# Attention and MLP on one core: score groups of each batch moved up by two groups, and the last half product cut in two column pieces

## The chip, the core and the metric

The kernel runs on one core of a Trainium2 chip. The core has five engines that run side by side, each with its own instruction queue worked in order: TensorE (PE) multiplies matrices into PSUM, VectorE (DVE) and ScalarE (ACT) work on PSUM and SBUF, GpSimd (POOL) casts here, and SyncE (SP) issues most of the DMAs. A DMA that SP, ACT or POOL issues waits in that engine's queue until what it reads is there, and holds all behind it. Times are device microseconds; the metric is the time of one execution.

## What is computed

```python
B, H, S, D = 8, 12, 448, 64
scores = q @ k.transpose(0, 1, 3, 2) / sqrt(D)
attn = softmax(scores)
x = (attn @ v).transpose(0, 2, 1, 3).reshape(B * S, H * D)
h = x @ w_in
g = maximum(0.01 * h, h)
out = g @ w_out
```

The inputs q, k, v (8 x 12 x 448 x 64), w_in (768 x 2048) and w_out (2048 x 768) and the output (3584 x 768) are float32. The kernel multiplies in bfloat16.

## The kernel before

**Units and groups.** The attention is cut into 48 units; unit u is one pair of heads of one batch, so six units make a batch. A unit has four chunks of 112 keys. For a chunk, `scores(u, c)` (L252) does two matmuls into one of three PSUM tiles `sc`, and `expo(u, c)` (L261) is one ACT instruction that writes the exponentials into one of three buffers `e`. `pv(u, j)` (L271) then multiplies the exponentials of head j with v in 16 matmuls, and DVE divides by the row sums (L278, L279) into a tile `x`. When both heads of a unit are done, `x_transposes(u)` turns the tile into the rows of `xT` that the MLP reads; from unit 9 on this is a DMA transpose on SP's queue (L213). Likewise the casted q and k of a unit (L146, on POOL) are turned into `qkT` by a DMA transpose from unit 14 on.

`cluster(g)` is a group: three chunks of scores, their exponentials (the third is held in `late` until the next call of `settle()`), the heads that are due, and the casts, loads and transposes of later units. Four groups are three units, so a batch has eight groups. `cluster` is called with `free` true or false; with false it places no heads and leaves them in `due`.

**Token ranges.** The MLP runs over eight ranges of tokens, i = 0 to 7, cut at multiples of 128: 384 tokens for even i, 512 for odd i. Range i needs `xT` of all of batch i. `mlp(i)` yields its steps one after the other: 16 input products (`part`, L326, six matmuls each, accumulated over the 128-row slices of `xT`, one slice per unit of the batch; ACT's leaky ReLU at L462 reads the bank), and then the output products. These are, for a pair of 128-token blocks, seven half-width products of eight matmuls (`block_pair`, L367; DVE prepares sums of h and of w_out, seven products take the place of eight), and for an odd block two full products (`blocks`, L427). Input and output products and `pv` share two PSUM banks, `g`, in turn (`next_bank`). In `block_pair` the two tiles `a` and `b` are these banks.

**What sets the order.** The order is written by hand; each engine's queue is what the loop at the end emits. `begin[i]` is the first group that is placed inside range i, and the groups `begin[i]` to `begin[i + 1] - 1` are spread over its steps in proportion to the matmul columns done (`catch_up`), after steps that yield true or false, not after those that yield None. So `begin` alone says how far the attention runs ahead of the MLP: batch i ends with group 8(i + 1) - 1, and range i starts in front of group `begin[i]`:

```python
begin = [9] + [8 * (i + 1) + 3 for i in range(1, B)]
```

The values are 9, 19, 27, 35, 43, 51, 59, 67: ten groups in range 0, eight in each of 1 to 6. The groups 64 to 66 have no scores, only heads that are due.

**Start of the last range.** For i = 7 two input products (m = 0 and m = 8) are opened ahead, five of six matmuls each, one in either bank (L456 to L458), and the first two steps add the sixth (L461).

**The end.** The very last product of the last block pair, the other half of block `o2`, is done in two pieces of 192 columns (L401 to L408), each followed by a DVE copy and two stores, one on ACT's queue (16 rows) and one on SP's (112 rows).

Of the kernel before, what the change touches and what calls it, by code (L numbers as in the profile page):

```python
# [16 lines left out]
def kernel(  # L17
# [11 lines left out]
    B, H, S, D = q.shape  # L29
# [5 lines left out]
    KD = DM // P  # L35
    MD = DF // P
    NW = DM // 2
# [3 lines left out]
    cuts = [((b * S) // P) * P for b in range(B)] + [B * S]  # L41
# [22 lines left out]
    def next_bank():  # L64

        banks.reverse()
        return banks[1]
# [19 lines left out]
    w_out_sb = w_pool.tile([P, MD, DM], BF16)  # L87
    MH = MD // 2
# [130 lines left out]
    def idle_slot():  # L219

        t = ps_s.tile([P, 2, 512], F32, name="sc", tag="sc")
        return t[:, 0], t[:, 1]
# [36 lines left out]
    def expo(u, c):  # L259
        e = e_sb[u % NE][:, :EL].rearrange("p (j c s) -> p j c s", j=2, c=NSC)  # L260
        nc.scalar.activation(e[:, :, c, :], sc_t.pop((u, c))[:SC, :, :S], AX.Exp, scale=scale)  # L261
# [34 lines left out]
    def store(o, t0, cols=slice(0, DM), queues=(nc.sync, nc.sync)):  # L296

        queues = list(queues)
        done = 0
        while done < P:  # L300
            b, j = divmod(t0 + done, S)
            so, p = divmod(j, SC)
            n = min(SC - p, P - done)
            dst = out[b * S:(b + 1) * S].rearrange("(p so) n -> so p n", so=NSC)
            queues.pop(0).dma_start(out=dst[so, p:p + n, cols], in_=o[done:done + n, cols])
            done += n
# [4 lines left out]
    def settle():  # L311
        while late:
            expo(*late.pop(0))

    open_t = {}
    opened = (0, 1)

    def part(i, m, kks, bank=None):

        n = cuts[i + 1] - cuts[i]  # L320
        at = cuts[i] % NX
        fresh = m not in open_t
        if fresh:
            open_t[m] = next_bank() if bank is None else bank
        for kk in kks:
            nc.tensor.matmul(  # L326
                open_t[m][:, :n], w_in_sb[:, kk, ts(m, P)], xT[:, kk, at:at + n],
                start=(fresh and kk == kks[0]), stop=(kk == KD - 1),
            )

    def mix_weights():

        for m in range(0, MH, 2):
            lo, hi = slice(m, m + 2), slice(MH + m, MH + m + 2)
            w11, w12 = w_out_sb[:, lo, :NW], w_out_sb[:, lo, NW:]
            w21, w22 = w_out_sb[:, hi, :NW], w_out_sb[:, hi, NW:]
            t1, t2, t3, t4 = (w_mix[:, x, lo] for x in range(4))
            for o, x, y in ((t1, w12, w11), (t2, w22, t1), (t3, w22, w12), (t4, w21, t2)):
                nc.vector.tensor_sub(o, x, y)
                yield  # L340

    def mix_h(h, m, nh):

        lo, hi = slice(m, m + 2), slice(MH + m, MH + m + 2)
        h11, h21 = h[:, lo, :nh], h[:, lo, nh:2 * nh]
        h12, h22 = h[:, hi, :nh], h[:, hi, nh:2 * nh]
        s2, s3, s4 = (h_mix[:, x, lo, :nh] for x in range(3))
        nc.vector.tensor_sub(s3, h11, h21)  # L348
        nc.vector.tensor_add(h21, h21, h22)
        nc.vector.tensor_sub(s2, h21, h11)  # L350
        nc.vector.tensor_sub(s4, h12, s2)

    def block_pair(i, h, c, nh):

        lo, hi = slice(0, MH), slice(MH, MD)
        one, two = ts(c, P), slice(nh + c * P, nh + (c + 1) * P)
        s2, s3, s4 = (h_mix[:, x, :, one] for x in range(3))
        t1, t2, t3, t4 = (w_mix[:, x] for x in range(4))
        left, right = slice(0, NW), slice(NW, DM)
        o1 = o_pool.tile([P, DM], F32, name="o")  # L360
        o2 = o_pool.tile([P, DM], F32, name="o")
        b, a = next_bank(), next_bank()

        def product(ps, x, w, first=False):
            settle()
            for m in range(MH):
                nc.tensor.matmul(  # L367
                    ps[:, :NW], x[:, m], w[:, m], start=(first and m == 0), stop=(m == MH - 1), skip_group_check=True,
                )
            return MH * NW  # L370

        def keep(o, at, ps):
            nc.vector.tensor_copy(o[:, at], ps[:, :NW])  # L373

        def join(o, at, ps):
            nc.vector.tensor_add(o[:, at], o[:, at], ps[:, :NW])  # L376

        done = product(b, h[:, lo, one], w_out_sb[:, lo, left], first=True)
        keep(o1, left, b)
        yield done, None  # L380
        done = product(a, h[:, hi, one], w_out_sb[:, hi, left], first=True)
        join(o1, left, a)
        yield done, None
        done = product(b, s2, t2)
        keep(o1, right, b)
        yield done, None
        done = product(a, h[:, lo, two], t1, first=True)
        keep(o2, right, a)
        yield done, False
        done = product(b, s3, t3)  # L390
        join(o2, right, b)
        yield done, None
        done = product(a, s4, w_out_sb[:, hi, right])
        join(o1, right, a)
        store(o1, cuts[i] + one.start)
        yield done, None
        t0 = cuts[i] + two.start
        if t0 + P == B * S:
            store(o2, t0, right)
            settle()  # L400
            for w in (slice(0, NW // 2), slice(NW // 2, NW)):  # L401
                for m in range(MH):
                    nc.tensor.matmul(  # L403
                        b[:, w], h[:, MH + m, two], t4[:, m, w], start=False, stop=(m == MH - 1),
                        skip_group_check=True,
                    )
                nc.vector.tensor_copy(o2[:, w], b[:, w])
                store(o2, t0, w, (nc.scalar, nc.sync))  # L408
        else:
            done = product(b, h[:, hi, two], t4)  # L410
            keep(o2, left, b)
            store(o2, t0)
        next_bank()
        yield done, True

    def blocks(i, h, todo):

        o = {}
        n = cuts[i + 1] - cuts[i]
        for c, w in todo:  # L420
            settle()
            if c not in o:
                o[c] = o_pool.tile([P, DM], F32, name="o")
            ps = next_bank()
            nw = w.stop - w.start
            for m in range(MD):
                nc.tensor.matmul(  # L427
                    ps[:, :nw], h[:, m, ts(c, P)], w_out_sb[:, m, w],
                    start=(m == 0), stop=(m == MD - 1),
                )  # L430
            nc.vector.tensor_copy(o[c][:, w], ps[:, :nw])
            t0 = cuts[i] + c * P
            if w.stop == DM:
                store(o.pop(c), t0)
            yield MD * nw, True

    def mlp(i):

        n = cuts[i + 1] - cuts[i]
        h = h_pool.tile([P, MD, 4 * P], BF16, name="h")  # L440
        if i == 0:
            for m in opened:
                part(i, m, (KD - 1,))
            for m in range(MD):
                if m not in opened:
                    part(i, m, range(KD))
                nc.scalar.activation(h[:, m, :n], open_t.pop(m)[:, :n], AX.Prelu, alpha=0.01)
                settle()
                yield KD * n, True
            yield from blocks(i, h, [(c, slice(w, w + NW)) for w in (0, NW) for c in range(n // P)])  # L450
            return

        nh = n // (2 * P) * P
        weights = mix_weights() if i == 1 else iter(())
        ready = []
        if i == B - 1:  # L456
            for m in (0, MH):
                part(i, m, range(KD - 1))  # L458
        for m in range(MD):
            mm = m // 2 + m % 2 * MH  # L460
            part(i, mm, (KD - 1,) if mm in open_t else range(KD))  # L461
            nc.scalar.activation(h[:, mm, :n], open_t.pop(mm)[:, :n], AX.Prelu, alpha=0.01)  # L462
            settle()
            if ready:
                mix_h(h, ready.pop(), nh)
            if m % 4 == 3:
                ready.append(m // 2 - 1)
            next(weights, None)
            yield KD * n, True
        mix_h(h, ready.pop(), nh)  # L470
        for c in range(2 * nh // P, n // P):
            yield from blocks(i, h, [(c, slice(0, NW)), (c, slice(NW, DM))])
        for c in range(nh // P):
            yield from block_pair(i, h, c, nh)
# [90 lines left out]
    a, b = idle_slot()  # L565
# [16 lines left out]
    cast(HP + 3)  # L582


    begin = [9] + [8 * (i + 1) + 3 for i in range(1, B)]

    early = [4, 6, 8, 10, 12, 14, 16, 18, 20, 22]
    for i in range(B):
# [6 lines left out]
        used, done, groups = 0, 0, 0  # L595
# [50 lines left out]
```

## Time and profile before

| | |
|---|---|
| median of three runs | 418.79 us (417.53 to 420.53) |
| the profiled execution, its own time | 418.34 us |
| its span, first to last instruction | 416.6 us |
| mean granted clock of TensorE | 0.992 |
| instructions in the span | 9157 |
| HBM read, written | 45.61 MB, 11.01 MB |

The profile is one execution. A row of the timeline gives start and length in us, engine, line, operation, out<-in with shapes, the count of instructions merged into it, and in brackets how long the engine was idle before and which instruction released it. Matmuls are pipelined and the end of one is modelled, so the length of a row of matmuls holds the drain of the last one; the chain of waits counts the pace alone. PEld is the load of a matmul's weights, which overlaps with matmuls. SPq and ACTq are the queues of those engines, where DMAs are issued.

### The profile page before, as it was taken

To read this page: it belongs to the slowest core of one execution; us is meant where nothing else is said; L and a number is where in the kernel's file an instruction comes from. 1 tells how busy PE (TensorE), PEld (TensorE's weight loads), DVE (VectorE), ACT (ScalarE), POOL (GpSimd) and SP (SyncE) were. 2 spreads that over 40 slices of the span, in tenths; PEclk is the share of its full clock that TensorE was granted. 3 is DMA by queue.
4 is the path that set the end of the run, shared out by engine and by line. 5 is a ranking of instruction groups with operands and counts; after the bars stand their busy time and mean duration, and the time that the engine had idled before them with its cause. 6 is when DMAs were issued, how large, how long until landed. Compare 5 with 4: busy or idle time off the path is not lost.

```text
span 416.6 us, 9157 instructions
## 1 busy us (share of the span) xinstructions
PE 397.6 (95%) x3672; PEld 228.8 (55%) x3672; DVE 170.1 (41%) x457; ACT 228.4 (55%) x324; POOL 109.0 (26%) x177
## 2 busy tenths in 40 slices
PE   8899999999998999989999799999999899999994
PEld 3566665645565666544555556554555456654463
DVE  2652433366543334423544234334344324333442
ACT  5998773576424884457542686447643388114300
POOL 8776655541112221311211313131211000000000
PEclk9999999999999999999999999999999999999998
DMA  8999999983558847862659848877356511130022
GB/s 127 198 201 204 202 199 115 245 199 89 134 161 187 183 112 171 221 145 70 166 130 194 172 100 189 206 186 122 101 124 175 121 35 24 49 89 0 2 76 76
DMA packets 96587, 57.23 MB, mean 137 GB/s; under 512 B 53281, under 2 KB 93089, under 8 KB 96545
## 3 DMA queue, kind: packets, MB, share of 16 engines
q1 hardware_dynamic: 76848, 44.15, 46.1%
q0 software_dynamic: 19392, 12.26, 20.6%
q8 instruction: 28, 0.46, 0.4%
q10 hardware_dynamic: 304, 0.25, 0.2%
q14 instruction: 15, 0.11, 0.1%
HBM read 45.61 MB, written 11.01 MB: 136 GB/s over the span
## 4 chain that ended last, share of the span: by engine, by line
PE 88%; DMA 7%; DVE 2%; issue 1%; POOL 1%; ACT 0%; DVEq 0%; ACTq 0%; POOLq 0%
PE g L326 34%; PE g L367 24%; PE g L271 11%; PE sc L252 9%; PE g L427 8%; DMA xT<-x 4%; DMA fk<-in_k_dram 2%; PE g L235 1%; DMA out_dram<-o 1%; DVE x L279 1%; PE g L292 1%; PE sc L326 0%; DVE rec L278 0%; PE g L403 0%; POOL fq L111 0%
## 5 line engine op out<-in xcount | busy, mean ns | idle before, releaser
L261 ACT ACTIVATE e<-sc 112x896 bf16<-112x896 f32 x192 | 165.7, 916 | 89.1 <-PE sc L252 88.6
L326 PE MATMUL g<-xT,w_in_sb 128*128 128x512 bf16 (+1 forms) x756 | 151.5, 354 | 9.5 <-DMA xT<-x 7.8
L326 PEld LDWEIGHTS <-w_in_sb 128*128 128x128 bf16 x768 | 72.9, 98 | 75.4 <-issue 12.3
L462 ACT ACTIVATE h<-g 128x512 bf16<-128x512 f32 (+1 forms) x112 | 61.7, 552 | 69.6 <-PE g L326 69.0
L271 PEld LDWEIGHTS <-e 112*128 112x128 bf16 x1536 | 56.4, 98 | 23.3 <-issue 14.8
L271 PE MATMUL g<-v,e 112*128 112x65 bf16 x1536 | 64.3, 195 | 0.3 <-ACT e L261 0.2
L278 DVE RECIPROCAL rec<-g 112x4 f32<-112x4 f32 x96 | 17.5, 182 | 80.5 <-PE g L271 52.0
L252 PE MATMUL sc<-qkT 64*128 64x448 bf16 x384 | 49.8, 356 | 0.4 <-DVE qkT L241 0.4
L146 POOL CAST qkb<-fq 112x512 bf16<-112x512 f32 x30 | 19.5, 651 | 116.0 <-DMA fq<-in_q_dram 69.7
L367 PEld LDWEIGHTS <-h 128*128 128x128 bf16 x344 | 33.5, 98 | 23.1 <-issue 1.2
L279 DVE TENSOR_TENSOR x<-g,rec 112x256 bf16<-112x256 f32 x96 | 40.8, 425 | 3.6 <-DVE rec L278 0.3
L148 POOL CAST v<-fv 112x512 bf16<-112x512 f32 x30 | 18.7, 622 | 71.7 <-PE g L271 62.6
L373 DVE COPY o<-g 128x384 f32<-128x384 f32 x43 | 24.0, 557 | 30.2 <-PE g L367 30.2
L367 PEld LDWEIGHTS <-hmix 128*128 128x128 bf16 x264 | 25.2, 98 | 19.4 <-issue 3.6
L427 PE MATMUL g<-w_out_sb,h 128*128 128x384 bf16 x192 | 32.5, 326 | 0.4 <-DVE x L279 0.3
L367 PE MATMUL g<-w_mix,hmix 128*128 128x384 bf16 x176 | 32.3, 326 | 0.0
L367 PE MATMUL g<-w_out_sb,h 128*128 128x384 bf16 x176 | 30.4, 326 | 0.8 <-DVE x L279 0.7
L367 PE MATMUL g<-w_mix,h 128*128 128x384 bf16 x168 | 30.7, 326 | 0.0
L376 DVE TENSOR_TENSOR o<-o,g 128x384 f32<-128x384 f32 x33 | 18.3, 554 | 28.4 <-PE g L367 28.4
L427 PEld LDWEIGHTS <-h 128*128 128x128 bf16 x192 | 18.5, 98 | 12.2 <-issue 0.5
L252 PEld LDWEIGHTS <-qkT 64*128 64x128 bf16 x384 | 13.9, 94 | 18.8 <-issue 9.5
L348 DVE TENSOR_TENSOR hmix<-h 128x512 bf16<-128x512 bf16 (+1 forms) x28 | 10.5, 376 | 30.2 <-ACT h L462 30.2
(50 smaller groups left out, 198.2 us busy)
## 6 DMA issues: line engine op xcount, KB each, us to landing
fk<-in_k_dram SPq DMA_DIRECT2D x31, 224.0 KB, 3.5
fq<-in_q_dram SPq DMA_DIRECT2D x30, 224.0 KB, 3.3
fv<-in_v_dram SPq DMA_DIRECT2D x30, 224.0 KB, 4.0
w_in_sb<-in_moe_w_in_dram POOLq DMA_DIRECT2D x4, 768.0 KB, 11.6
w_out_sb<-in_moe_w_out_dram POOLq DMA_DIRECT2D x4, 768.0 KB, 13.4
out_dram<-o SPq DMA_DIRECT2D x7, 336.0 KB, 3.3
out_dram<-o SPq DMA_DIRECT2D x8, 288.0 KB, 3.1
out_dram<-o SPq DMA_DIRECT2D x8, 240.0 KB, 3.1
```

The lines of the kernel that those rows point to most:

```text
L146: by(qk_sb[u][:, x].rearrange("p so h d -> p h so d"), f)
L148: by(v_sb[u % NV][:, :, :, :D], f)
L252: nc.tensor.matmul(ps[:, j, :S], t[j * D:(j + 1) * D, S + c * SC:S + c * SC + P], t[j * D:(j + 1) * D, :S], start=True, stop=True,)
L261: nc.scalar.activation(e[:, :, c, :], sc_t.pop((u, c))[:SC, :, :S], AX.Exp, scale=scale)
L271: nc.tensor.matmul(ps[:, qc, :], e[:, at:at + P], vt[:, j, c, :], start=(c == 0), stop=(c == NSC - 1),)
L279: nc.vector.tensor_mul(x_t[u][:, :, j, :], ps[:SC, :, :D], rec.to_broadcast([SC, NSC, D]))
L326: nc.tensor.matmul(open_t[m][:, :n], w_in_sb[:, kk, ts(m, P)], xT[:, kk, at:at + n], start=(fresh and kk == kks[0]), stop=(kk == KD - 1),)
L367: nc.tensor.matmul(ps[:, :NW], x[:, m], w[:, m], start=(first and m == 0), stop=(m == MH - 1), skip_group_check=True,)
L373: nc.vector.tensor_copy(o[:, at], ps[:, :NW])
L376: nc.vector.tensor_add(o[:, at], o[:, at], ps[:, :NW])
L427: nc.tensor.matmul(ps[:, :nw], h[:, m, ts(c, P)], w_out_sb[:, m, w], start=(m == 0), stop=(m == MD - 1),)
L462: nc.scalar.activation(h[:, mm, :n], open_t.pop(mm)[:, :n], AX.Prelu, alpha=0.01)
```

## The change

```diff
@@ block_pair
-        done = product(a, s4, w_out_sb[:, hi, right])
-        join(o1, right, a)
-        store(o1, cuts[i] + one.start)
-        yield done, None
         t0 = cuts[i] + two.start
         if t0 + P == B * S:
             store(o2, t0, right)
-            settle()
-            for w in (slice(0, NW // 2), slice(NW // 2, NW)):
+
+            def piece(w):
+                settle()
                 for m in range(MH):
                     nc.tensor.matmul(
                         b[:, w], h[:, MH + m, two], t4[:, m, w], start=False, stop=(m == MH - 1),
                         skip_group_check=True,
                     )
+
+            def put(w):
                 nc.vector.tensor_copy(o2[:, w], b[:, w])
                 store(o2, t0, w, (nc.scalar, nc.sync))
-        else:
-            done = product(b, h[:, hi, two], t4)
-            keep(o2, left, b)
-            store(o2, t0)
+
+            piece(slice(0, NW // 2))
+            put(slice(0, NW // 2))
+            done = product(a, s4, w_out_sb[:, hi, right])
+            join(o1, right, a)
+            store(o1, cuts[i] + one.start)
+            piece(slice(NW // 2, NW))
+            put(slice(NW // 2, NW))
+            return
+        done = product(a, s4, w_out_sb[:, hi, right])
+        join(o1, right, a)
+        store(o1, cuts[i] + one.start)
+        yield done, None
+        done = product(b, h[:, hi, two], t4)
+        keep(o2, left, b)
+        store(o2, t0)
         next_bank()
         yield done, True
@@ mlp
-        if i == B - 1:
-            for m in (0, MH):
-                part(i, m, range(KD - 1))
         for m in range(MD):
             mm = m // 2 + m % 2 * MH
-            part(i, mm, (KD - 1,) if mm in open_t else range(KD))
+            part(i, mm, range(KD))
@@ the loop at the end
-    begin = [9] + [8 * (i + 1) + 3 for i in range(1, B)]
+    begin = [9, 8 * 2 + 3] + [8 * (i + 1) + 5 for i in range(2, B - 1)] + [8 * B + 3]
```

`begin` is now 9, 19, 29, 37, 45, 53, 61, 67. Range 1 holds ten groups (19 to 28) where it held eight, ranges 2 to 5 hold eight each, all two groups further on, and range 6 holds six (61 to 66). The two products opened ahead of range 7 are gone. The last block pair's order becomes: left piece, the product for the other block, right piece.

**The end of range 1 on SP's queue.** `x_1951` is unit 17, the last of batch 2, which range 2 reads, and `x_2105` is unit 18; `o_1965` and `o_1966` are the output blocks of the second block pair of range 1. Before:

```order
L305 DMA out_0_dram<-o_1965 48x768 [waits DMAHW1_49,DVE_49]
L305 DMA out_0_dram<-o_1965 80x768 [waits DMAHW2_49]
L305 DMA out_0_dram<-o_1966 16x768 [waits DMAHW3_49,DVE_49]
L305 DMA out_0_dram<-o_1966 112x768 [waits DMAHW4_49]
L213 DMA_TRANSPOSE xT_114<-x_1951 128x4x112 [waits DMAHW5_49,DVE_49]
L213 DMA_TRANSPOSE xT_114<-x_2105 128x4x112 [waits DMAHW6_49,DVE_49]
```

After, on the same queue, unit 17 is `x_1962`, unit 18 is `x_2025`, and the second block pair's stores begin with `o_2071`:

```order
L213 DMA_TRANSPOSE xT_114<-x_1962 128x4x112 [waits DMAHW5_49,DVE_49]
L122 DMA fq_2001<-in_q_dram 112x2x256 [waits DMAHW6_49]
L122 DMA fk_2003<-in_k_dram 112x2x256 [waits DMAHW7_49]
L122 DMA fv_2005<-in_v_dram 112x2x256 [waits DMAHW0_49,Pool_49]
L213 DMA_TRANSPOSE qkT1_111<-qkb_1904 128x8x112 [waits DMAHW1_49,PE_49,Pool_49]
L213 DMA_TRANSPOSE xT_114<-x_2025 128x4x112 [waits DMAHW2_49,DVE_49]
L122 DMA fq_2064<-in_q_dram 112x2x256 [waits DMAHW3_49]
L122 DMA fk_2066<-in_k_dram 112x2x256 [waits DMAHW4_49]
L122 DMA fv_2068<-in_v_dram 112x2x256 [waits DMAHW5_49,Pool_49]
L213 DMA_TRANSPOSE qkT2_112<-qkb_1997 128x8x112 [waits DMAHW6_49,PE_49,Pool_49]
L213 DMA_TRANSPOSE qkT3_113<-qkb_2060 128x8x112 [waits DMAHW7_49,PE_49,Pool_49]
L305 DMA out_0_dram<-o_2071 48x768 [waits DMAHW0_49,DVE_49]
```

Unit 17's transpose moved from behind the stores of the second block pair to a place ahead of them, and unit 18's with it; the loads of two units and two transposes of q and k moved up in the same way.

**Between the two block pairs of range 1 on PE.** Of each run of matmuls the first row is shown; `sc` is a chunk's scores, `e` and `v` the product of a head, L367 the block pairs. Before, after the first block pair:

```order
L271 MATMUL g1_100<-v4_105,e1_108 128x65 [waits Pool_49]
L252 MATMUL sc_1904<-qkT2_112 128x448 [waits Activation_49]
L252 MATMUL sc_1907<-qkT2_112 128x448 [waits Activation_49]
L252 MATMUL sc_1910<-qkT2_112 128x448 [waits Activation_49]
L271 MATMUL g0_99<-v4_105,e1_108 128x65 [waits DVE_49]
L271 MATMUL g1_100<-v5_106,e2_109 128x65 [waits Pool_49]
L367 MATMUL g0_99<-w_out_sb_116,h_1455 128x384 [waits DVE_49]
```

After, at the same place:

```order
L271 MATMUL g1_100<-v5_106,e2_109 128x65 [waits Pool_49]
L252 MATMUL sc_1966<-qkT2_112 128x448 [waits Activation_49]
L252 MATMUL sc_1969<-qkT3_113 128x448 [waits Activation_49]
L252 MATMUL sc_1972<-qkT3_113 128x448 [waits Activation_49]
L271 MATMUL g0_99<-v5_106,e2_109 128x65 [waits DVE_49]
L271 MATMUL g1_100<-v0_101,e0_107 128x65 [waits Pool_49]
L252 MATMUL sc_2029<-qkT3_113 128x448 [waits PE_49]
L252 MATMUL sc_2032<-qkT3_113 128x448 [waits Activation_49]
L252 MATMUL sc_2035<-qkT0_110 128x448 [waits Activation_49]
L271 MATMUL g0_99<-v0_101,e0_107 128x65 [waits DVE_49]
L367 MATMUL g1_100<-w_out_sb_116,h_1455 128x384 [waits DVE_49]
```

Where one group stood between the block pairs, two now stand back to back (groups 25 and 26), each with three chunks and two heads.

**The last stores on SP's queue.** `o_5435` is the block o1 of the last pair and `o_5436` its block o2; 384 columns are o2's right half and 192 a piece. Before:

```order
L305 DMA out_0_dram<-o_5435 48x768 [waits DMAHW1_49,DVE_49]
L305 DMA out_0_dram<-o_5435 80x768 [waits DMAHW3_49]
L305 DMA out_0_dram<-o_5436 16x384 [waits DMAHW5_49]
L305 DMA out_0_dram<-o_5436 112x384 [waits DMAHW6_49]
L305 DMA out_0_dram<-o_5436 112x192 [waits DMAHW7_49,DVE_49]
L305 DMA out_0_dram<-o_5436 112x192 [waits DMAHW0_49,DVE_49]
```

After:

```order
L305 DMA out_0_dram<-o_5436 16x384 [waits DMAHW1_49,DVE_49]
L305 DMA out_0_dram<-o_5436 112x384 [waits DMAHW2_49]
L305 DMA out_0_dram<-o_5436 112x192 [waits DMAHW4_49,DVE_49]
L305 DMA out_0_dram<-o_5435 48x768 [waits DMAHW5_49,DVE_49]
L305 DMA out_0_dram<-o_5435 80x768 [waits DMAHW7_49]
L305 DMA out_0_dram<-o_5436 112x192 [waits DMAHW0_49,DVE_49]
```

The two stores of o1 moved from ahead of all of o2's to a place between its left and its right piece.

## The prediction

> **What bounds the kernel now.** I read the busy table of the page first, then the table of waits, then the timeline at the places that the waits name, then busy time by stretches, and last the tail. The first two give the frame.
>
> ```profile
> PE 397.6 (95%) x3672; PEld 228.8 (55%) x3672; DVE 170.1 (41%) x457; ACT 228.4 (55%) x324; POOL 109.0 (26%) x177
> PE g L326 <- DMA xT<-x: 7.8, 5, 2.0
> PE 88%; DMA 7%; DVE 2%; issue 1%; POOL 1%; ACT 0%; DVEq 0%; ACTq 0%; POOLq 0%
> ```
>
> The first row says that TensorE (PE) is busy for 397.6 of the 416.6 us span, so at most 19 us can be won without removing matmuls, and this change removes none. The second row is the largest wait of PE on anything: five times the matmuls of line 326 (the input product of the MLP) wait for a transposed tile x, 7.8 us in all. In the third row, the chain of waits, DMA is what is left beside PE. The timeline shows the five waits, and a sixth, smaller one with another releaser:
>
> ```profile
> 134.36 1.30 PE L326 MATMUL g<-xT,w_in_sb 128*128 128x384 bf16 x7 [1.40 <-DMA xT<-x]
> 179.26 1.67 PE L326 MATMUL g<-xT,w_in_sb 128*128 128x512 bf16 x7 [1.81 <-DMA xT<-x]
> 233.28 1.30 PE L326 MATMUL g<-xT,w_in_sb 128*128 128x384 bf16 x7 [1.96 <-DMA xT<-x]
> 277.14 1.67 PE L326 MATMUL g<-xT,w_in_sb 128*128 128x512 bf16 x7 [0.78 <-DMA xT<-x]
> 331.03 2.15 PE L326 MATMUL g<-xT,w_in_sb 128*128 128x384 bf16 x7 [1.85 <-DMA xT<-x]
> 374.50 3.83 PE L326 MATMUL g<-xT,w_in_sb 128*128 128x512 bf16 x17 [0.52 <-ACT h L462]
> ```
>
> Each of the five stands in the first product of a batch's MLP (batches 2 to 6): the first five matmuls run, the sixth needs the columns of the last head pair. Why that pair is late can be read on the SP queue and PE at the first of them:
>
> ```profile
> 128.77 2.08 SPq L305 DMA_DIRECT2D out_dram<-o  x4
> 129.90 0.74 PE L252 MATMUL sc<-qkT 64*128 64x448 bf16 x6
> 130.36 1.73 ACT L261 ACTIVATE e<-sc 112x896 bf16<-112x896 f32 x2 [2.66 <-PE sc L252]
> 130.95 2.75 SPq L213 DMA_TRANSPOSE xT<-x  x2
> 131.99 0.97 PE L326 MATMUL g<-xT,w_in_sb 128*128 128x384 bf16 x5 [0.22 <-DVE x L279]
> xT<-x SPq DMA_TRANSPOSE x39, 2.5
> ```
>
> The transpose goes out at 130.95, behind four output stores, and lands some 2.5 us or more later (the median of all 39, last row); PE asks for it at 132.96. Between such places PE is full:
>
> ```profile
> 134.40:175.00 40.60, 40.60 (x393) 24.32 (x393) 15.83 (x45) 26.03 (x39) 9.34 (x16) 1.00 0.73 166
> 331.10:334.50 3.40, 3.40 (x27) 2.06 (x28) 0.30 (x2) 1.79 (x3) 0.00 (x0) 0.53 0.35 68
> 79.00:130.00 51.00, 50.78 (x432) 27.43 (x430) 28.74 (x67) 29.05 (x40) 11.40 (x17) 1.00 0.68 159
> ```
>
> Columns are the stretch and its length, then busy time of PE, weight loads, DVE, ACT, POOL, the granted clock, DMA share and GB/s. In the first row PE idles for nothing at clock 1.00, while ACT is busy 26.03 of 40.6 us (64%). The second row follows the fifth wait: the granted clock is 0.53 for 3.4 us, a loss of 3.4 x 0.47 = 1.6 us which the waits table does not show.
>
> **The change, part by part.** *The five waits.* Two groups move from later token ranges into range 1, so every later range starts two groups further on in the attention. The pair that was late is now finished earlier: for range 2 the transpose of unit 17 stands ahead of all four products-and-stores of the second block pair, instead of behind them. A pair is seven products of eight matmuls, and a product takes 16.99/104 x 8 = 1.31 us:
>
> ```profile
> 392.79 16.99 PE g L367 x104
> ```
>
> So the transpose gets more than 9 us of matmuls before it is wanted, against 2 us now; a landing of 2.5 us has room four times over. The same holds for the other four ranges: the last unit's second half is finished either in an output block or after the first pair, and never just before the range starts. I take the whole 1.40 + 1.81 + 1.96 + 0.78 + 1.85 = 7.8 us off. What is late next there is the PSUM bank, 0.22 us in the row at 131.99; the same three consecutive head products stand there afterwards, so it stays and I book nothing.
>
> *The slow stretch.* It begins with the resumption after a 1.85 us gap. All the other stretches into which I cut the time from 10 to 411.7 us, sixteen of them, have a granted clock of 1.00; the first and the last:
>
> ```profile
> 10.00:26.40 16.40, 15.02 (x253) 9.93 (x252) 10.60 (x31) 15.96 (x20) 12.98 (x21) 1.00 1.35 199
> ...
> 392.80:411.70 18.90, 18.45 (x120) 11.33 (x118) 8.77 (x17) 0.60 (x1) 0.00 (x0) 1.00 0.17 47
> ```
>
> Four other gaps, one of them 1.96 us, were followed by no slow stretch, so whether a gap cools the clock depends on more than its length; but without gaps I expect none. 1.6 us off. The Trainium skill, "TensorE: Matmul & The Clock Gate", section "Why this matters for your kernels", warns of gaps above about 3 us, one idle window. Its half-rate state agrees with the 0.53 here, its gap length does not: 1.85 us was enough. By that rule the gap would not be the cause, the stretch would remain and the sum would come out 1.6 us higher; the same possibility is a rival below, worked out from the rows.
>
> *The opened parts of the last range.* Ten matmuls that ran ahead into both banks are put back in plain order; the count is the same. The cover that they gave was for the last transpose, and unit 47 is finished before the last block pair in both orders, some 9 us ahead. What goes is the 0.52 us wait at 374.50, where the second opened bank blocks the third product. 0.5 us off.
>
> *Range 1 is denser: ten groups instead of eight.* Its ACT work was 29.05 us of 51.0 and grows by 2 x 3 exponentials; the two in the row at 130.36 take 1.73, so 0.87 each, 5.2 us more, while PE grows by some 2 x 1.6 us. That is 34 of 54 us, no bound. But after its first block pair two groups now stand back to back. PE there has: 16 matmuls of a head (0.62), six of scores (0.67), a head, a head, scores, a head. The score buffers hold three chunks, so the second group's scores wait for the first group's exponentials:
>
> ```profile
> 129.97 0.67 PE sc L252 x6
> 136.85 0.62 PE g L271 x16
> ACT e L261 <- PE sc L252: 88.6, 39, 5.3
> ```
>
> With the first score matmul at 0.62, the exponentials start 0.46 later as in the rows at 129.90 and 130.36 and end at 2.00, 2.86 and 3.73. PE is ready for the second group's second chunk at 2.75 and waits 0.16, until 0.05 behind the second end; it is ready for the third at 3.13 and waits until 3.78, another 0.65. I add 0.8 us. It could be zero if PE ran later than this, or three full exponentials, 2.6 us, if ACT were behind already; 2.66 us of ACT idle ahead of the row at 130.36 speaks against that.
>
> *Starts of ranges 2 to 6.* The third group's scores there used to follow a head product; now they come directly after the second input product, so the third chunk may wait for the exponential that was held back behind the first activation:
>
> ```profile
> 134.77 0.49 ACT L462 ACTIVATE h<-g 128x384 bf16<-128x384 f32 x1 [2.68 <-PE g L326]
> 135.16 0.91 ACT L261 ACTIVATE e<-sc 112x896 bf16<-112x896 f32 x1
> 179.72 0.60 ACT L462 ACTIVATE h<-g 128x512 bf16<-128x512 f32 x1 [3.41 <-PE g L326]
> 180.22 0.91 ACT L261 ACTIVATE e<-sc 112x896 bf16<-112x896 f32 x1
> ```
>
> From the end of the first input product: activation 0.25 later, exponential 0.39 after it, 0.91 long, 0.05 to release: 1.60. PE wants the buffer after the second product and two chunks, 0.97 + 0.45 = 1.42, for the 384-token ranges: 0.18 us each, 0.5 for three. For the 512-token ranges (third and fourth row, 0.50 apart) 1.30 + 0.45 = 1.75 is later than 1.71, so none. The ends are 0 and one exponential in all five, 4.6.
>
> *SP, POOL and DMA queues.* Loads, casts and transposes of q and k move with their groups and keep their order among themselves. At the double group two casts and two transposes come close together; the transposed q and k are used a full pair, 9 us, later. The waits table has no wait of PE for a q or k transpose, so there is slack; I book zero.
>
> *The tail.* The order becomes left piece, other product, right piece.
>
> ```profile
> 404.42 1.46 PE L367 MATMUL g<-w_mix,hmix 128*128 128x384 bf16 x8
> 404.62 0.55 DVE L376 TENSOR_TENSOR o<-o,g 128x384 f32<-128x384 f32 x1 [0.74 <-PE g L367]
> 408.32 1.46 PE L367 MATMUL g<-w_out_sb,hmix 128*128 128x384 bf16 x8
> 410.48 0.36 DVE L407 COPY o<-g 128x192 f32<-128x192 f32 x1
> 410.89 0.82 PE L403 MATMUL g<-w_mix,h 128*128 128x192 bf16 x8 [0.45 <-DVE o L407]
> 409.78 0.67 PE g L403 x8
> 411.75 0.36 DVE L407 COPY o<-g 128x192 f32<-128x192 f32 x1 [0.91 <-PE g L403]
> 412.84 0.37 SPq L305 DMA_DIRECT2D out_dram<-o  x1
> SPq L641 <- DMA out_dram<-o: 1.9, 1, 1.9
> out_dram<-o SPq DMA_DIRECT2D x8, 240.0 KB, 3.1
> ```
>
> The right piece loses its wait for the copy of the left one (410.84 to 410.89), because a product now lies between. But the left piece accumulates into the bank that the addition of the product just before still reads: that addition starts 0.2 after the bank's last matmul and takes 0.55, so the left piece starts at 408.32 + 0.75 + 0.05 = 409.12, then 0.67, 1.31, and the right piece begins at 411.10 instead of 410.89. Its copy ends 0.2 later, at 412.3. The stores of the other block, two issues of about 0.4, now start at its addition's end, 411.85, so SP reaches the last store at 412.7, not 412.84; but the larger store ahead of it, issued at 412.3, lands 3.1 later, at 415.4, against 415.1 (412.84 + 0.37 + 1.9) now. I add 0.3; the ends are -0.1 (issue alone decides) and +1.
>
> **The sum.** The profiled execution took 418.34 us, span 416.6 and 1.74 around it. 418.34 - 7.8 - 1.6 - 0.5 + 0.8 + 0.5 + 0.3 = 410.0. The median of the three runs shown is 418.79, 0.1% above that execution.
>
> **Rivals.** *The slow stretch stays, or another place cools* (the left piece's wait in the tail and the double group are new gaps): 410.0 + 1.6 = 411.6. For it: the 1.96 us gap did nothing, so the gap may not be the cause. Against: the only slow stretch follows a gap at once. Chance 0.15.
>
> *ACT takes over at the range starts.* The PE gaps gave ACT idle time (2.68 us in the row at 134.77). If its backlog binds once they go, each of the five starts pays one exponential, 0.91 instead of 0.18 or nothing, and the double group its 2.6 in place of 0.8: 410.0 + 4.1 + 1.8 = 415.9, and half of it 413. Against: 64% ACT load in the stretch without gaps. Chance 0.12, half of it on either side of 1%.
>
> *The change does not do what it says*: PE waits for a transpose still, because SP reaches it late behind stores or casts; nothing gained but the 0.5, 418. Against: the order puts the transpose ahead of a whole pair. Chance 0.05.
>
> *Slower: q and k transposes come late.* The first transposes pass the stores, and SP works in order, so a transposed x that waits for DVE, or a q that waits for POOL, holds all behind it. If the scores of the 35 groups from 29 to 63 then waited for their q and k, the gain of 8.3 would be eaten at 0.24 us a group, and 1% above the median of before, 423.0, reached at 0.37. It needs the slack that now leaves no such wait in the table to vanish; chance 0.04.
>
> **Numbers.** The forecast has 0.64. Its own bounds: all added costs zero, 408.4, and the bank waits may go too, 5 x 0.22, 407.3; added costs doubled, 411.6. With the slow stretch on top 413.2, which also takes in the nearer half of the ACT case: the range is 407.4 to 413.5. A measurement of this kernel tells about 1% from no change, so faster means under 414.6: 0.64 + 0.15 + 0.06 = 0.85; same 0.06 + 0.05 = 0.11; slower 0.04.
>
> **What would show it.** Right: no row with PE waiting for xT at a range start, granted clock 1.00 through the middle, PE waiting on ACT for some 0.8 us once in range 1, and on DVE for 0.8 us before the left piece in the tail. Wrong: new rows of PE waiting on ACT or on qkT of over 2 us together, a slow stretch elsewhere, or a tail more than 1 us longer.

## The result, and the profile after

| | before | after |
|---|---|---|
| median | 419.66 us (417.53 to 422.16, 4 runs) | 408.11 us (407.76 to 408.24, 4 runs) |
| the profiled execution | 418.34 us | 408.24 us |
| its span | 416.6 us | 406.5 us |
| mean granted clock | 0.992 | 0.997 |

The ratio of the runs is 0.9721, with an interval of 0.9663 to 0.9779: 2.8% faster. The forecast was 410.0. Not only the time fell, but its scatter: 0.5 us over four runs against 4.6. Ratios here and below leave out the few runs that lie over 1.5% above the fastest of the same kernel, while medians and ranges hold all runs.

The mean clock has to be read with care, because it also counts the time behind the last matmul. In the profile after, the clock is full up to 403.96 us and half (0.50) from there to the end, when no matmul is left; that alone makes 0.997. In the profile before, half of the missing 0.008 is such an end of 3.3 us, and the other half is the slow stretch.

The busy table, the table of waits of TensorE (PE) and the chain of waits of the changed kernel:

```profile
PE 393.6 (97%) x3655; PEld 228.4 (56%) x3672; DVE 173.0 (43%) x457; ACT 228.3 (56%) x324; POOL 110.0 (27%) x177
PE g L185 <- DVE gate L179: 1.2, 1, 1.2
PE g L326 <- DVE x L279: 1.1, 5, 0.2
PE g L235 <- DVE qkb L146: 0.9, 1, 0.9
PE g L400 <- DVE o L376: 0.6, 1, 0.6
PE sc L252 <- DVE qkT L241: 0.6, 2, 0.4
PE sc L252 <- ACT e L261: 0.4, 1, 0.4
PE 92%; DVE 3%; ACT 1%; DMA 1%; issue 1%; DVEq 0%; ACTq 0%; POOLq 0%
```

The row that led the table before, PE waiting for a transposed x, is gone altogether; PE's idle time went from 19.0 to 12.9 us, and DMA in the chain from 7% to 1%. (The profile after holds 17 matmul records fewer, 3655 of 3672, so the 12.9 is a little too high.) Two rows are new, the wait on ACT for `e` and the one at line 400 on the addition. The start of range 2 shows how the place that waited looks now, in the timeline:

```profile
133.06 0.74 PE L252 MATMUL sc<-qkT 64*128 64x448 bf16 x6
133.74 1.20 PE L271 MATMUL g<-v,e 112*128 112x65 bf16 x32
135.15 2.11 PE L326 MATMUL g<-xT,w_in_sb 128*128 128x384 bf16 x12 [0.22 <-DVE x L279]
136.71 0.91 ACT L261 ACTIVATE e<-sc 112x896 bf16<-112x896 f32 x1
137.20 0.84 PE L252 MATMUL sc<-qkT 64*128 64x448 bf16 x6
```

Twelve matmuls of line 326 run without a break where there were five, a gap and seven. The 0.22 us on the bank stays, as booked. The next scores take 0.84 us instead of 0.74: their third chunk waits 0.10 for the exponential that ends at 137.62. Such a short wait falls into the drain of the matmul before it and is not in the table of waits.

Between the block pairs of range 1 the two groups stand back to back:

```profile
118.10 0.67 PE L271 MATMUL g<-v,e 112*128 112x65 bf16 x16
118.71 0.74 PE L252 MATMUL sc<-qkT 64*128 64x448 bf16 x6
119.17 4.96 ACT L261 ACTIVATE e<-sc 112x896 bf16<-112x896 f32 x6 [2.66 <-PE sc L252]
119.38 1.35 PE L271 MATMUL g<-v,e 112*128 112x65 bf16 x32
120.66 0.65 PE L252 MATMUL sc<-qkT 64*128 64x448 bf16 x4
121.75 0.36 PE L252 MATMUL sc<-qkT 64*128 64x448 bf16 x2 [0.44 <-ACT e L261]
122.05 0.68 PE L271 MATMUL g<-v,e 112*128 112x65 bf16 x16
122.57 2.76 PE L367 MATMUL g<-w_out_sb,h 128*128 128x384 bf16 x16
```

From 118.10 to 122.57 are 4.47 us; without a wait it would be four heads of 0.62 and two times 0.67 of scores, 3.82. The double group cost 0.65. In return a wait is gone that the kernel before had ahead of the same second block pair: 0.22 us for the bank at 119.41 in its timeline.

And the tail:

```profile
396.64 1.46 PE L367 MATMUL g<-w_mix,hmix 128*128 128x384 bf16 x8
398.14 0.55 DVE L376 TENSOR_TENSOR o<-o,g 128x384 f32<-128x384 f32 x1 [0.74 <-PE g L367]
398.75 0.82 PE L400 MATMUL g<-w_mix,h 128*128 128x192 bf16 x8 [0.65 <-DVE o L376]
399.41 1.46 PE L367 MATMUL g<-w_out_sb,hmix 128*128 128x384 bf16 x8
400.71 0.82 PE L400 MATMUL g<-w_mix,h 128*128 128x192 bf16 x8
401.57 0.36 DVE L406 COPY o<-g 128x192 f32<-128x192 f32 x1
SPq L649 <- DMA out_dram<-o: 2.3, 1, 2.3
```

The left piece waits for the addition that reads its bank, the right piece waits for nothing. The last row, SP's waits, is the wait for the last store, 2.3 us against 1.9 before.

### The profile page after: what moved, and what is told of

Read it like the earlier page. It is cut to its first block, busy times and chain, and to the rows that moved or that the text cites. A ratio compares the mean times of both kernels' runs of the same rounds, so it can differ in the third digit from the quotient of the medians.

```text
span 406.5 us, 9142 instructions
## 1 busy us (share of the span) xinstructions
PE 393.6 (97%) x3655; PEld 228.4 (56%) x3672; DVE 173.0 (43%) x457; ACT 228.3 (56%) x324; POOL 110.0 (27%) x177
## 4 chain that ended last, share of the span: by engine, by line
PE 92%; DVE 3%; ACT 1%; DMA 1%; issue 1%; DVEq 0%; ACTq 0%; POOLq 0%
PE g L326 35%; PE g L367 25%; PE g L271 12%; PE sc L252 10%; PE g L438 8%; PE g L235 1%; ACT e L261 1%; DVE x L279 1%; DMA fq<-in_q_dram 1%; PE g L292 1%; DVE rec L278 1%; PE sc L326 0%; PE g L400 0%; DVE xT L293 0%; DVE qkb L146 0%
## 5 line engine op out<-in xcount | busy, mean ns | idle before, releaser
L326 PE MATMUL g<-xT,w_in_sb 128*128 128x384 bf16 (+1 forms) x739 | 148.8, 352 | 2.2 <-DVE x L279 1.1
L146 POOL CAST qkb<-fq 112x512 bf16<-112x512 f32 x30 | 18.6, 621 | 111.0 <-DMA fq<-in_q_dram 82.9
L367 PEld LDWEIGHTS <-h 128*128 128x128 bf16 x344 | 33.4, 98 | 22.7 <-issue 0.6
L367 PEld LDWEIGHTS <-hmix 128*128 128x128 bf16 x264 | 25.1, 98 | 19.3 <-issue 3.6
L367 PE MATMUL g<-w_mix,hmix 128*128 128x384 bf16 x176 | 32.3, 326 | 0.0
L367 PE MATMUL g<-w_out_sb,h 128*128 128x384 bf16 x176 | 30.4, 326 | 0.4 <-DVE x L279 0.4
L367 PE MATMUL g<-w_mix,h 128*128 128x384 bf16 x168 | 30.7, 326 | 0.0
L348 DVE TENSOR_TENSOR hmix<-h 128x512 bf16<-128x512 bf16 (+1 forms) x28 | 11.8, 420 | 31.5 <-ACT h L470 31.5
```

Source lines behind the costliest of these rows:

```text
L146: by(qk_sb[u][:, x].rearrange("p so h d -> p h so d"), f)
L326: nc.tensor.matmul(open_t[m][:, :n], w_in_sb[:, kk, ts(m, P)], xT[:, kk, at:at + n], start=(fresh and kk == kks[0]), stop=(kk == KD - 1),)
L367: nc.tensor.matmul(ps[:, :NW], x[:, m], w[:, m], start=(first and m == 0), stop=(m == MH - 1), skip_group_check=True,)
```

## Experiments

Each of the three sets has its own runs of the kernel before, and the changed kernel or the one before again as a yardstick.

**The changed kernel once more** (no edit).

> The changed kernel once more, as the yardstick of this set. Theory (gaps and the clock that followed them are gone): 408.1 us, all runs within 0.5 us of each other, mean granted clock 0.997 or above in each. Rival (the slow stretch comes by itself, gap or no gap): single runs 1.6 us or more above the others, with a clock near 0.993.

408.63 us (408.29 to 408.84), clocks 0.997 to 0.999 in all six runs. No run stands out by 1.6 us.

**The transpose held back.**

```diff
-        if j == 1 and a >= NXP:
+        if j == 1 and a in (17, 23, 29, 35, 41):
+            held.append(a)
+        elif j == 1 and a >= NXP:
             x_transposes(a)
...
+        if g + 1 in begin[2:7]:
+            while held:
+                x_transposes(held.pop(0))
         t, r = divmod(g, 4)
```

The pool of x tiles has six buffers instead of three here, so that a held tile can stay.

> The changed kernel with one thing put back: the transpose of the last unit of batches 2 to 6 (units 17, 23, 29, 35, 41) is held until the last group in front of the range that reads it, behind the stores of the pair, where the kernel before had it; groups, ranges and the tail stay as changed. Theory (the gain is the late transpose): five waits of PE for xT come back, 8.6 us by the pace of the matmuls, and with them slow stretches of 0 to 3 times 1.6 us: 417 to 421 us, spread of the runs over 1 us. Rival (the gain comes from the new spacing of the groups, the denser range 1 and lighter range 6): 408 us, no change.

421.12 us (418.71 to 425.16), at the upper end of the theory; the kernel before in the same set 419.22, ratio 1.003 (0.9998 to 1.0063). The whole gain is given back, with the new groups, ranges and tail in place. Its table of waits, and its first range start:

```profile
PE g L326 <- DMA xT<-x: 9.3, 5, 2.8
132.11 2.09 SPq L305 DMA_DIRECT2D out_dram<-o  x4
134.25 3.04 SPq L213 DMA_TRANSPOSE xT<-x  x2
135.32 0.97 PE L326 MATMUL g<-xT,w_in_sb 128*128 128x384 bf16 x5 [0.22 <-DVE x L279]
138.66 2.40 PE L326 MATMUL g<-xT,w_in_sb 128*128 128x384 bf16 x7 [2.37 <-DMA xT<-x]
```

The five waits are back, and the scatter with them. That settles the cause: it is the late issue of the transpose, not the spacing of the groups.

It does not say what made the issue late in the kernel before. There the stores ahead of it on SP's queue are the smaller part. At the first range start the x tile itself was ready only at 130.64, by this row of the kernel before:

```profile
130.22 0.42 DVE L279 TENSOR_TENSOR x<-g,rec 112x256 bf16<-112x256 f32 x1
```

Its transpose went out at 130.95, 0.31 us later. At the other four range starts the same difference is 0.33, 0.31, 0.34 and 0.60 us. So waiting behind the stores accounts for at most 1.9 us of the five waits together; the rest is that the last head of the batch stood right in front of the range that reads it. The change moved both.

**The old tail in the changed kernel.** The lines of the tail are those of before.

> The changed kernel with the tail of the kernel before: the other block's product ahead of both pieces. Theory (the new tail trades a 0.45 us wait for the copy for a 0.65 us wait for the addition and ends 0.3 us later): 407.8 us, 0.3 below the changed kernel. Rival (the new tail is a gain, since o2's left piece is stored earlier): 408.4 us or more.

407.89 us (407.63 to 408.44), 0.74 below the yardstick of 408.63. The direction is the theory's, the size more than twice; but the changed kernel's own medians lie between 408.11 and 408.63, so the size is not certain from runs alone.

**The opened products back in the changed kernel.**

```diff
+        if i == B - 1:
+            for m in (0, MH):
+                part(i, m, range(KD - 1))
```

> The changed kernel with the two input products of the last range opened ahead again. Theory (they block the third product on the bank, by 0.6 us): 408.7 us, with the 0.5 us wait of PE on ACT at the start of range 7 back. Rival (they cover a late transpose or cost nothing): 408.1 us or less.

409.18 us (408.84 to 409.76), 0.55 above the yardstick, and the 0.52 us wait of PE on ACT at the start of range 7 is back in its profile. They were a cost.

**The kernel before once more** (no edit).

> The kernel before once more, for its scatter. Theory (each gap may or may not be followed by a stretch at half clock, by where it falls): times spread over 1.5 us or more, and the granted clock falls with the time, about 1.6 us for each 0.004 of mean clock. Rival (the scatter is in the loads of the start or in DMA): times spread at one and the same clock.

420.28 us (417.93 to 423.32). Over the 46 executions of the kernel before in the first two sets, those with a mean clock of 0.994 or more have a median of 418.2 us (14), of 0.989 to 0.993 one of 420.5 (20), of 0.988 or less one of 420.9 (12); a straight line through them gives 1.3 us for 0.004 of clock, with a correlation of -0.76. So a good part of the scatter goes with the clock, although the mean clock also holds the half clock of the end, which costs nothing; the waits themselves vary too, 10.0 us in this profile against 7.8:

```profile
PE g L326 <- DMA xT<-x: 10.0, 5, 3.1
180.94 3.15 PE L326 MATMUL g<-xT,w_in_sb 128*128 128x512 bf16 x7 [3.08 <-DMA xT<-x]
236.42 1.30 PE L326 MATMUL g<-xT,w_in_sb 128*128 128x384 bf16 x7 [1.94 <-DMA xT<-x]
```

The 512-column row that follows the 3.08 us gap takes 3.15 us where it takes 1.67 at full clock: the slow stretch of this execution is at range 3, not at range 6.

**The new numbers of the first groups alone**, in the kernel before.

```diff
-    begin = [9] + [8 * (i + 1) + 3 for i in range(1, B)]
+    begin = [9, 8 * 2 + 3] + [8 * (i + 1) + 5 for i in range(2, B - 1)] + [8 * B + 3]
```

> The kernel before with the new numbers of the first groups alone: old tail, opened products kept. Theory: the five waits and the slow stretches go, all else as before: 408.1 + 0.6 (opened products) - 0.3 (old tail) = 408.4 us. Rival (a good part of the gain is the tail or the last range's start): 410 us or more.

408.81 us (408.12 to 409.4) against 420.14, ratio 0.9748 (0.9714 to 0.9781). This one line is the gain. The time is 0.4 above the theory's 408.4, so differences of half a microsecond between versions are not resolved by these runs.

**One group of lead instead of two.**

```diff
-    begin = [9, 8 * 2 + 3] + [8 * (i + 1) + 5 for i in range(2, B - 1)] + [8 * B + 3]
+    begin = [9, 8 * 2 + 3] + [8 * (i + 1) + 4 for i in range(2, B - 1)] + [8 * B + 3]
```

> The changed kernel with the ranges 2 to 6 one group further on than before instead of two: range 1 holds nine groups and range 6 seven. The last unit of a batch is then finished between the block pairs, or in an output block, as with two; no two groups stand back to back in range 1. Theory (a transpose that is one pair, 9 us, ahead is early enough, and the double group costs 0.65): 407.5 us. Rival (the second group of lead matters): above 409 us, with PE waiting for xT again.

406.78 us (406.13 to 407.3), 1.3 to 1.9 below the changed kernel's medians of 408.11 to 408.63. One group of lead is enough: PE waits for no transpose. It gained more than the 0.65 of the double group. The chain of waits of the changed kernel (its second execution) has two pieces between range 1 and range 6 that are absent here, in front of the second pairs of ranges 3 and 5, besides the double group's:

```profile
120.06 1.73 ACT e L261 x2
216.87 0.19 DVE rec L278
217.09 0.44 DVE x L279
311.84 0.19 DVE rec L278
312.06 0.43 DVE x L279
```

There three heads precede a product, one ahead of a group's scores and two back to back behind them, and the product waits for its bank, 0.4 us each: 0.22 in the table, which counts from the modelled end of the matmul before, and 0.16 more by the pace of the matmuls. With one group of lead only two heads stand there, one on either side of the scores. 0.65 + 0.8 is 1.45; the rest, up to 0.4, is within the scatter between sets. The two bank waits are no cost of the change: the kernel before has them too, 0.22 us each at 217.77 and 315.63, besides the one in range 1. One group of lead removes all three.

**The last product whole.**

```diff
-            piece(slice(0, NW // 2))
-            put(slice(0, NW // 2))
             done = product(a, s4, w_out_sb[:, hi, right])
             join(o1, right, a)
             store(o1, cuts[i] + one.start)
-            piece(slice(NW // 2, NW))
-            put(slice(NW // 2, NW))
+            done = product(b, h[:, hi, two], t4)
+            keep(o2, left, b)
+            store(o2, t0, left, (nc.scalar, nc.sync))
```

> The changed kernel with the last half product whole: other block's product first, then eight matmuls of 384 columns, one copy of 384 columns, and its two stores on ACT's and SP's queues. Theory (each cut of the last product has cost a wait on the bank of 0.45 to 0.65, more than the shorter copy saves): PE ends 1.31 after the other block's product where the old cut takes 0.67 + 0.6 + 0.67, the copy takes 0.56 instead of 0.36, so 0.4 earlier than the old tail: 407.4 us. Rival (a smaller last store lands sooner and pays for the cut): 408 us or more.

407.63 us (407.29 to 407.99): below the changed kernel by 0.5 to 1.0, by which of its medians one takes, and by 0.26 below the old tail, in another set, which the runs alone don't tell apart. The profiles do. From the start of the last matmul of `g<-w_mix,hmix`, behind which all three tails have the same work, to the end of the span are 8.13 to 8.40 us in the five profiles with the old tail, 8.66 to 8.86 in the seven with the new one, and 7.72 and 7.78 in the two with the whole product. So it is better than the cut in either order. PE ends with no wait between the last two products:

```profile
398.23 1.46 PE L367 MATMUL g<-w_out_sb,hmix 128*128 128x384 bf16 x8
399.53 1.46 PE L367 MATMUL g<-w_mix,h 128*128 128x384 bf16 x8
401.03 0.56 DVE L373 COPY o<-g 128x384 f32<-128x384 f32 x1 [0.75 <-PE g L367]
```

**The yardstick of the third set** (the changed kernel, no edit).

> The changed kernel as the yardstick of this set: 408.1 to 408.6 us, as in the two sets before.

408.51 us (407.94 to 410.18). The run of 410.18 lies 1.6 us above the next one and has the lowest clock of the six, 0.995. That is what one slow stretch would look like; its profile was not kept, so it is not shown.

**Range 1's groups apart.**

```diff
+        if i == 1:
+            total *= 0.92
```

> The changed kernel with the groups of range 1 a little closer together (its total times 0.92), so that the groups 25 and 26 stand on either side of the second half of the first block pair and not back to back. Theory (the double group costs PE 0.65 us, but the three heads in a row that come instead cost the 0.4 us bank wait that ranges 3 and 5 have): 0.25 us below the changed kernel. Rival (the double group costs nothing, or more than its row shows): the same time, or more than 0.8 us below.

408.46 us (407.89 to 409.25), no difference. The expectation was missed, and the run doesn't tell the two apart: the double group is gone, but two waits of PE came in its place in range 1, on the copy and on the bank:

```profile
112.74 1.46 PE L367 MATMUL g<-w_mix,hmix 128*128 128x384 bf16 x8 [0.44 <-DVE o L373]
122.72 2.76 PE L367 MATMUL g<-w_out_sb,h 128*128 128x384 bf16 x16 [0.22 <-DVE x L279]
```

With 0.16 of drain each they are 0.60 and 0.38, about what was saved. The second is the wait that the kernel before had at this place. The price of the double group thus rests on its own rows.

**One group of lead and the whole last product.**

> One group of lead (as in shift_one) and the whole last product (as in whole_tail). Theory (the two touch different places and add up): 406.8 - 1.0 = 405.8 us, 2.6 below the changed kernel. Rival (the tail's gain was in the scatter between sets): 406.5 us or more.

405.47 us (404.74 to 406.63), 3.0 below the yardstick of its set, and 0.9678 (0.9637 to 0.9719) of the kernel before. The two add up, within the scatter between sets. This version beats both kernels.

**Work put into the gaps of the kernel before.**

```diff
+            if m == 0 and 2 <= i < B - 1:
+                part(i, mm, range(KD - 1))
+                for _ in range(24):
+                    nc.tensor.matmul(banks[0][:, :P], warm[:, :P], warm[:, :P], start=True, stop=True)
             part(i, mm, (KD - 1,) if mm in open_t else range(KD))
```

> The kernel before, with 24 matmuls of 128 columns on zeros between the fifth and the sixth matmul of the first input product of ranges 2 to 6, written into the bank that the next product overwrites: work that fills some 1.3 us of each gap. Theory (the idle time of PE is what lets the clock fall): clock of 0.996 or above in nearly all runs, 417 us, spread under 2 us, some 2 to 3 us below the kernel before, though nothing of the waiting is gone. Rival (the slow stretches come by themselves or from the transposes): clocks down to 0.988 as before and 420 us.

418.56 us against 419.35, ratio 0.9991 (0.9963 to 1.0018): no difference, the expected 2 to 3 us are not there. The clock was 0.996 or more in 9 of 12 executions, against 7 of 16 of the kernel before in this set, and 12 of 46 in the two sets ahead. The spread was 4.1 us, not under 2. In the profile the clock is 1.00, but the filler was as long as some gaps and other gaps stayed:

```profile
132.33 1.50 PE L464 MATMUL g<-warm 128*128 128x128 bf16 x24
134.12 1.30 PE L326 MATMUL g<-xT,w_in_sb 128*128 128x384 bf16 x7 [0.29 <-DMA xT<-x]
233.59 1.30 PE L326 MATMUL g<-xT,w_in_sb 128*128 128x384 bf16 x7 [1.80 <-DMA xT<-x]
```

So the clock leans to the theory and the time doesn't confirm it. Among the runs with a clock of 0.996 or more, the median is 418.5 us with the filler and 418.4 without, so the filler can save no more than what the slow stretches cost, and in this set that was under 1 us.

## Why the prediction was right, term by term

The forecast of 410.0 was 1.9 above the median. The profiled executions differ by 10.1 us of span where the sum had 8.3; by landmarks in the chain of waits of both, with the same work between them. Those of the changed kernel:

```profile
78.28 0.67 PE sc L252 x6
361.69 1.51 PE g L326 x7
382.41 15.71 PE g L367 x96
```

The last row ends at 398.12, ahead of the cut; before, the same point is 1.31 ahead of the end of the row of 104 matmuls, at 408.47.

| part | predicted | measured |
|---|---|---|
| start, up to the last scores of range 0 (78.70 and 78.28) | 0 | -0.4 |
| from there to the first product of range 7 (371.39 and 361.69) | -8.1 | -9.3 |
| range 7 up to the products ahead of the cut | -0.5 | -0.7 |
| tail, to the end of the span | +0.3 | +0.3 |

*The five waits* (-7.8). The mechanism was right: holding the transpose back returned the whole gain, and the first-group numbers alone gave it. The size was too small, and this is the term that was mis-sized most. The idle time in the table starts at the modelled end of the matmul before, drain included. At the first wait the fifth matmul starts at 131.99 + 4 x 0.163 = 132.64, the pace would put the sixth at 132.80, it came at 134.36: 1.56 lost, and the row says 1.40. Over the five places that is 8.6 us and not 7.8.

*The slow stretch* (-1.6). Right in this execution, and shown in the runs as scatter: with the gaps gone, the clock was 0.995 or above in all 58 executions of versions without them, and the times of one version in one set lie within 0.5 to 2.3 us. No profile of such a version has a slow stretch between its matmuls, so the rival that it stays is refuted as far as these runs go, but for the one run of 410.18 us.

What starts it is not the length of a gap: the gaps that were followed by one were 1.85, 2.37 and 3.08 us long (one in each of three profiles), and gaps of 1.94, 1.96 and 2.84 were not. In these profiles it is where the gap falls. In the three the half clock lasts 3.41 us and starts 95, 51 and 39 times 3.413 us after the clock first became full. Cut from that moment on into stretches of 3.413 us, the profiles can be read by how long PE was busy in a stretch (the third figure, with the clock as the third from the end). The first two rows are from the kernel before, around its 1.85 us gap; the last two from the held transposes, around the 2.84 us gap:

```profile
327.91:331.32 3.41, 1.34 (x10) 0.67 (x7) 0.76 (x3) 0.40 (x1) 0.00 (x0) 1.00 0.74 168
331.32:334.74 3.41, 3.41 (x29) 1.94 (x26) 0.54 (x2) 1.88 (x4) 0.00 (x0) 0.50 0.34 66
234.12:237.53 3.41, 1.91 (x35) 1.33 (x32) 1.12 (x4) 1.26 (x2) 0.62 (x1) 1.00 1.36 184
237.53:240.95 3.41, 1.85 (x13) 0.88 (x12) 0.00 (x0) 1.45 (x3) 0.52 (x1) 1.00 0.71 206
```

The 1.85 us gap and the wait just ahead of it fell into one stretch and left PE 1.34 us of work; the next stretch ran at half clock. The 2.84 us gap was divided between two stretches with 1.91 and 1.85, and the clock stayed full. All 14 profiles agree: behind each of the 16 stretches with 1.43 us of work or less the clock was half (three between matmuls, the others at the end of an execution), and behind none of the 1632 with 1.60 or more. In the profile with work put into the gaps, the lowest stretch between matmuls has 1.61. The stretches start at another time in each execution (7.06, 6.52 and 5.43 us in these three), so the same gaps are followed by a slow stretch in one and not in the next. The prediction's statement that more than the length decides was right.

*The opened products* (-0.5). Right: 0.55 by the run that put them back.

*The double group* (+0.8). 0.65 by its rows. The run that was to isolate it did not. Not booked was that the bank wait of 0.4 us ahead of the second pair of range 1 goes with it.

*The third chunk at range starts* (+0.5). 0.4: the scores there take 0.84, 0.89 and 0.89 us at the starts of ranges 2, 4 and 6 and 0.74 elsewhere, as the row of range 2 above and these of ranges 4 and 6 show; the 512-token ranges have no such row:

```profile
232.11 0.89 PE L252 MATMUL sc<-qkT 64*128 64x448 bf16 x6
327.08 0.89 PE L252 MATMUL sc<-qkT 64*128 64x448 bf16 x6
```

*The tail* (+0.3). The wait for the addition came as booked, 0.65 in the table and 0.8 by the pace, and the last store took 2.3 instead of 1.9 us after its issue. The two profiles agree with +0.3, and over all profiles the tail is 0.4 longer (medians 8.78 and 8.38, counted as under "The last product whole"); the runs of one set say 0.74. The term was right in its mechanism and, by the profiles, in its size.

With the start's 0.4, which the change doesn't touch, and the bank wait of range 1, -8.6 - 1.6 - 0.7 + 0.65 - 0.4 + 0.4 + 0.3 - 0.4 gives -10.35, against -10.1; the 0.25 between them is not assigned.

*The rivals.* ACT didn't take over: PE waited 0.4 us on it by the table, and another 0.4 at the range starts. No wait for q or k transposes came up.

## What to carry to other kernels

A wait that stands at the start of each stage is worth its idle time, the drain that the table hides, and what the clock does behind it; moving its producer one step ahead, together with the DMA that carries it, was enough, and the second step of lead only brought bunched groups. Before a product is cut to shorten the tail, ask what reads the bank that the piece goes on writing: both cuts paid a wait of 0.45 to 0.65 us, more than they saved, and the tail with the whole product was shorter than either. Where a kernel's runs scatter, look at the clock of each run: the gaps that cost time may also be what makes it scatter.

## What the runs showed of the hardware

The half clock came after gaps of 1.85 and 2.37 us, and not after one of 2.84, so the length of a gap alone doesn't decide; how much of one 3.41 us stretch it empties does, in every profile here (1.43 us of work or less against 1.60 or more). The Trainium skill, "TensorE: Matmul & The Clock Gate", section "Why this matters for your kernels", names gaps above about 3 us, of which the profiles show only one between matmuls, 3.08 us, with a slow stretch behind it. The slow stretch of the kernel before moved between executions from range 6 to range 3. I had not expected one kernel's DMA transposes at the same place to land so differently from one execution to the next: PE waited for the same one 1.81 us in one profile and 3.08 in the other.
